# Attention mixed with a spectral filter: the score tiles lend one PSUM bank each instead of two, the last chunk's transposes move from PSUM to SBUF, and the order of the work is planned anew

## The chip, the cores and the metric

The kernel runs on one core of one Trainium2 chip. The number that counts is the device time of one execution in microseconds (us), and less is better. A core has engines that run side by side, each with its own queue of instructions that it works off strictly in order: PE (TensorE, matrix products into PSUM), ACT (ScalarE), DVE (VectorE), POOL (GpSimd) and SP, which here issues most DMAs. They wait for each other through semaphores. PSUM is the memory that PE writes; the kernel uses all of its eight banks of 128 x 512 float32.

## The reference

For an input `x` of 2048 tokens with 448 features, the result is `g * a + (1 - g) * b`, token by token:

```python
g = sigmoid((x * gate_w).sum(-1, keepdims=True))
qkv = (x @ wqkv).reshape(B, S, 3, 16, 28)             # 16 heads of 28 features
scores = einsum("bhqd,bhkd->bhqk", q, k) * 28 ** -0.5
a = (softmax(scores) @ v) @ wo                         # full attention, no mask
X = rfft2(x.astype(float32), axes=(-2, -1))
b = irfft2(X * (w_r + 1j * w_i), s=(2048, 448)).astype(bfloat16)
```

All inputs are bfloat16, and so is the result.

## The kernel before

**Attention.** The heads stand in four groups of four (`g`), the queries in four blocks of 512 (`qc`). One pair is a **chunk**, so there are 16, worked off one after the other; the last has `g` = 3 and `qc` = 3. A chunk has 64 **units**: 16 blocks of 128 keys times four heads. For each unit PE makes a 128 x 512 block of scores (L1166), one of two engines turns it into weights, and PE adds `V` times the weights into the bank `psV` (L1249). One round of scores (`scores`) fills one of the two tiles `psA0` and `psA1`, which have **two banks each**; ACT then makes the exponentials of both banks with one instruction of 128 x 1024 (L1189). When DVE has room, the round takes a third or fourth unit into single banks `psX0` to `psX2`; DVE turns those into weights by an integer method (the "z" at L1212, which fills an SBUF tile `P`, and two "shifts" of the tile at L1232, on DVE or POOL, each of which fills a further `P`). Before the values of such a unit are complete, PE uses all three.

**The other work** goes between these rounds: the projections of queries, keys and values, the forward and inverse transforms, and at the end the output tiles. All of it lands in the banks `psX`, and `take_bank` hands out whichever is free. `spare` lists further banks that may be lent: `psV` and the banks of the `psA` tiles. They are lent while the exponentials have not started, and the `psA` banks again when the last scores are out: an exponential that ends after that puts its tile's banks on the free list (`add_exp`, in `done`).

**The end of the program.** There are 16 output tiles of 128 tokens, t = 4 `qc` + b. A tile needs 20 matmuls of 32 x 448 into one bank: four for each of the four head groups (`Wo` against `qT`, which holds the normalised attention by then), and four that add the transform (`bufA`). It is then scaled and copied to SBUF (L865 on DVE, L867 on ACT; tiles `fin0` to `fin3`, and for t = 12 to 15 the halves of `T12_0` and `T12_1`) and stored by a DMA. Tiles 12 to 15 are **late**: 16 of their matmuls are made ahead, and the four of the last head group follow when chunk 15 is normalised. That last step is `finale`: DVE transposes `psV` in two halves of 256 columns, takes reciprocals of the sums, multiplies them by the odds of the gate, multiplies the halves by the result, and transposes back into `qT3_3` (L1361 to L1370). The transposed halves lie in two `psX` banks that are taken for good. While `finale` is under way (`self.final`), DVE takes no other work, so output tiles are scaled by ACT. POOL's last work is the 16 sums and 16 differences of the inverse transform that fill `bufA` (L826, L828).

**What sets the order.** Nothing in the program text does. `plan` runs a small event-driven model of the engines while the program is built: each engine, when free, takes the ready step with the best priority, with the rules of `pick`, `dispatch` and `want_D`. The numbers in `TUNE` are due times and thresholds of those rules. The instructions are then written in the order in which the model started them, so any change of a rule, of a bank or of a number can reorder everything behind it. A tile framework adds the semaphore waits, by the tiles that an instruction reads and writes.

Of the kernel before, what the change touches and what calls it, by code (L numbers as in the profile page):

```python
# [16 lines left out]
ALU = mybir.AluOpType  # L17
# [11 lines left out]
ONE = DH  # L29
# [139 lines left out]
class Unit:  # L169
    __slots__ = ("bank",)  # L170

    def __init__(self):
        self.bank = None


TUNE = dict(T0=14686.546, LC=22185.379, late=11458.875, pzmin=5, urg=6, lastd=1, dt1=1308.304, dt2=934.424, minx2=1,
            poolt=7236.982, th=152.929, pw=94.522, pt=5990.959, ph=174.007, slack=205.092, q0a=0.939, q0b=0.915, q0n=1.28,
            v0=1.985, v1=0.481, vr=0.337, va=4.36, vb=0.452, kb=-3.17, ks=0.299, kn=-2.187, qb=-1.855, qs=0.176, qn=-2.498,
            gate=-0.848, fo=0.11, fos=0.629, fa=1.907, fas=0.25, sp=2.701, sps=4189.909, fc=7.462, fcs=0.275, fp=11.206,
            fps=0.212, fsd=44318.209, ow=15952.526, ows=2033.1, u8=-4896.554, u12=21653.512, relx=-4760.365, mc=46.01)  # L180

ENGINES = ("PE", "ACT", "DVE", "POOL", "SP")
LAT = {"PE": 230.0, "ACT": 170.0, "DVE": 150.0, "POOL": 80.0, "SP": 0.0}
# [12 lines left out]
class Kernel:  # L196
# [522 lines left out]
    def transform(self, at):  # L719
# [161 lines left out]
    def plan(self):  # L881
        self.order = []
        self.out_d = {}
        self.norm_d = {}
        self.late = {}
        self.norms = []
        self.seq = 0
        self.evq = []
        self.now = 0.0
        self.free_at = {e: 0.0 for e in ENGINES}  # L890
        self.port_until = 0.0
        self.ready = {e: [] for e in ENGINES}
# [48 lines left out]
        left = [o.name for o in self.ops if not o.started and o.engs]  # L941
        assert not left, (t, self.pos, self.pv, left[:30])
# [244 lines left out]
    def add_exp(self, p, us, i, slot):  # L1187
        n = len(us)
        e = self.op("exp", {"ACT": t_act(QW * n)}, lambda o: self.nc.scalar.activation(  # L1189
            out=self.P[slot][:, 0:n, :], in_=self.PSA[i][:, 0:n, :], func=ACT.Exp, scale=math.log(2.0) / UNIT), [p], -1e9)  # L1190
# [159 lines left out]
    def finale(self, p, g, qc):  # L1350

        nc = self.nc
        n0 = len(self.ops)
        self.final = 2
        for h in range(2):
            u = Unit()
            u.bank = self.take_bank()
            cs = slice(256 * h, 256 * h + 256)
            R, tmp = self.Rsm[h][:].rearrange("p j b -> p (j b)")[:, 0:8], self.nq[h][:, 0:256]
            blk = lambda x: x.rearrange("p (c d) -> p c d", d=32)  # L1360
            e = self.ev(f"t1{h}", {"DVE": 340.0}, lambda e, u=u, cs=cs: nc.vector.transpose(out=u.bank[:, 0:256], in_=self.PSV[:, cs]),  # L1361
                        [p], -2e9 + 10 * h)
            e = self.ev(f"t2{h}", {"DVE": 130.0}, lambda e, u=u, R=R: nc.vector.reciprocal(
                out=R, in_=u.bank[:, ONE:256:32]), [e], -2e9 + 10 * h + 1)
            e = self.ev(f"t3{h}", {"DVE": 70.0}, lambda e, R=R, h=h: nc.vector.tensor_tensor(
                out=R, in0=R, in1=self.oddsT[:, 1, 8 * h:8 * h + 8], op=ALU.mult), [e, self.o_oddsT], -2e9 + 10 * h + 2)
            e = self.ev(f"t4{h}", {"DVE": 340.0}, lambda e, u=u, R=R, tmp=tmp: nc.vector.tensor_tensor(
                out=blk(tmp), in0=blk(u.bank[:, 0:256]), in1=R.rearrange("p (c o) -> p c o", o=1).to_broadcast([128, 8, 32]), op=ALU.mult),
                [e], -2e9 + 10 * h + 3)
            e = self.ev(f"t5{h}", {"DVE": 340.0}, lambda e, cs=cs, tmp=tmp: nc.vector.transpose(  # L1370
                out=self.qT[g][qc][:, cs], in_=tmp), [e], -2e9 + 10 * h + 4)
            e.kind = "t5"
            self.finals(qc, h, e)
        self.wake(n0)
# [47 lines left out]
```

## Time and profile before

| what | value |
|---|---|
| time, median of 3 runs | 378.99 us (377.62 to 381.48) |
| the profiled execution's own time | 378.07 us |
| its span, first to last instruction | 376.3 us |
| ACT busy | 359.7 us (96%) |
| PE busy | 354.2 us (94%) |
| DVE busy | 333.5 us (89%) |
| POOL busy | 259.2 us (69%) |
| TensorE clock granted, mean | 1.000 |

The profile is of one execution. Between its span and its time lie 1.8 us outside the first and last instruction. Engines overlap, so shares do not add up to one; what an engine's work is worth depends on whether another waits for it. Instructions of ACT and DVE are pipelined: one starts before the one ahead has ended, so the step from start to start is shorter than the duration of one.

### The profile page before, as it was taken

To read this page: it belongs to the slowest core of one execution; us is meant where nothing else is said; L and a number is where in the kernel's file an instruction comes from. 1 tells how busy PE (TensorE), PEld (TensorE's weight loads), DVE (VectorE), ACT (ScalarE), POOL (GpSimd) and SP (SyncE) were. 2 spreads that over 40 slices of the span, in tenths; PEclk is the share of its full clock that TensorE was granted. 3 is DMA by queue.
4 is the path that set the end of the run, shared out by engine and by line. 5 is a ranking of instruction groups with operands and counts; after the bars stand their busy time and mean duration, and the time that the engine had idled before them with its cause. 6 is when DMAs were issued, how large, how long until landed. Compare 5 with 4: busy or idle time off the path is not lost.

```text
span 376.3 us, 13601 instructions
## 1 busy us (share of the span) xinstructions
PE 354.2 (94%) x5656; PEld 132.8 (35%) x5656; DVE 333.5 (89%) x604; ACT 359.7 (96%) x403; POOL 259.2 (69%) x292
## 2 busy tenths in 40 slices
PE   7999999999999999999989999999989889999994
PEld 5552224335333343233333333232324323332342
DVE  1679999999999999999999999998999989999970
ACT  4999999999999999999999999999999999999962
POOL 5555677766777865668766678687778876775780
PEclk9999999999999999999999999999999999999999
DMA  8701120211855532202212212112100100101012
GB/s 239 163 3 4 5 36 4 60 22 46 99 63 89 75 58 38 57 3 67 53 48 57 64 46 60 47 29 68 31 17 17 24 11 2 33 13 54 26 64 75
DMA packets 43493, 18.55 MB, mean 49 GB/s; under 512 B 29876, under 2 KB 41580, under 8 KB 43432
## 3 DMA queue, kind: packets, MB, share of 16 engines
q1 hardware_dynamic: 42680, 17.54, 23.0%
q8 instruction: 44, 0.72, 0.9%
q10 hardware_dynamic: 752, 0.15, 0.2%
q14 instruction: 17, 0.14, 0.1%
HBM read 13.71 MB, written 2.07 MB: 42 GB/s over the span
## 4 chain that ended last, share of the span: by engine, by line
PE 60%; ACT 24%; DVE 9%; issue 4%; DMA 1%; POOL 0%; SPq 0%; ACTq 0%; DVEq 0%
ACT P L1189 23%; PE psA L1166 21%; PE psX L355 20%; PE psV L1249 16%; DVE P L1212 5%; PE psA L355 2%; DVE P L1232 1%; DMA bufA<-in_A_x_dram 1%; PE psX L458 1%; POOL P L1232 0%; PE psX L1166 0%; DVE kT L557 0%; ACT fin L867 0%; DVE Oraw L367 0%; DVE VT L834 0%
## 5 line engine op out<-in xcount | busy, mean ns | idle before, releaser
L1189 ACT ACTIVATE P<-psA 128x1024 bf16<-128x1024 f32 x379 | 348.8, 1125 | 1.1 <-PE psX L1166 1.1
L1232 POOL TENSOR_SCALAR P<-P 128x1024 int16<-128x1024 int16 (+1 forms) x164 | 168.5, 1029 | 64.8 <-DVE P L1232 22.6
L1212 DVE TENSOR_SCALAR P<-psX 128x512 int16<-128x512 f32 x267 | 177.6, 684 | 14.5 <-PE psX L1166 12.1
L1166 PE MATMUL psA<-qT,kT 32*128 32x512 bf16 x757 | 146.5, 383 | 12.2 <-ACT P L1189 10.8
L1249 PE MATMUL psV<-P,V 128*32 128x512 bf16 x1558 | 129.9, 384 | 0.9 <-DVE P L1212 0.7
L1166 PE MATMUL psX<-qT,kT 32*128 32x512 bf16 x267 | 93.4, 384 | 0.0
L1166 PEld LDWEIGHTS <-kT 32*128 32x128 bf16 x1024 | 41.6, 91 | 133.3 <-issue 129.5
L1249 PEld LDWEIGHTS <-V 128*32 128x32 bf16 x1558 | 32.7, 94 | 45.5 <-issue 41.3
L1232 DVE TENSOR_SCALAR P<-P 128x1024 int16<-128x1024 int16 (+1 forms) x108 | 45.3, 422 | 0.4
L355 PE MATMUL psX<-xT,Wp 112*32 112x512 bf16 (+2 forms) x528 | 40.7, 377 | 0.5 <-ACT xT L370 0.5
L1313 POOL TENSOR_TENSOR qT<-Oraw,Rbc 128x512 bf16<-128x512 f32 x14 | 17.9, 1277 | 3.2 <-DVE P L1232 2.0
L789 DVE TENSOR_TENSOR T<-psX,Wst 128x900 bf16<-128x900 f32 x16 | 17.3, 1084 | 0.2
L355 PEld LDWEIGHTS <-Wp 112*32 112x32 bf16 x528 | 11.0, 94 | 14.4 <-issue 12.3
L746 POOL TENSOR_TENSOR VT<-bufA 128x900 bf16<-128x900 bf16 x8 | 14.4, 1794 | 1.8 <-DVE P L1232 1.1
L355 PEld LDWEIGHTS <-xT 112*32 112x32 bf16 x768 | 12.6, 96 | 6.9 <-issue 6.4
L797 POOL TENSOR_TENSOR bufA<-T 128x225 bf16<-128x225 bf16 x16 | 9.8, 613 | 6.0 <-DVE P L1232 5.5
L355 PEld LDWEIGHTS <-VT 113*32 113x32 bf16 (+2 forms) x512 | 10.0, 95 | 8.8 <-issue 8.1
L355 PE MATMUL psX<-IV,bufA 128*32 128x256 bf16 (+1 forms) x256 | 12.2, 275 | 0.2 <-DVE P L1212 0.2
L355 PE MATMUL psX<-Wo,qT 128*32 128x448 bf16 x160 | 12.3, 356 | 0.0
L795 POOL TENSOR_TENSOR bufA<-T 128x225 bf16<-128x225 bf16 x16 | 9.0, 562 | 4.5 <-PE psX L1166 2.2
L826 POOL TENSOR_TENSOR bufA<-bufB 128x225 bf16<-128x225 bf16 x16 | 9.3, 583 | 3.7 <-DVE P L1232 2.9
L834 DVE CAST VT<-psX 113x512 bf16<-113x512 f32 x16 | 10.8, 676 | 1.0 <-PE psX L355 1.0
(106 smaller groups left out, 288.2 us busy)
## 6 DMA issues: line engine op xcount, KB each, us to landing
Rbc<-dR SPq DMA_DIRECT2D x14, 256.0 KB
IV<-c_IV SPq DMA_DIRECT2D x16, 128.0 KB
bufA<-bufB SPq DMA_DIRECT2D x16, 112.5 KB
S<-c_S SPq DMA_DIRECT2D x16, 96.0 KB
bufA<-in_A_x_dram SPq DMA_DIRECT2D x3, 448.0 KB
out_dram<-fin SPq DMA_DIRECT2D x12, 112.0 KB
Wst<-in_B_w_r_dram SPq DMA_DIRECT2D x7, 112.5 KB
Wst<-in_B_w_i_dram SPq DMA_DIRECT2D x7, 112.5 KB
```

The costliest lines, as they stand in the source:

```text
L355: self.nc.tensor.matmul(o[c:c + n], lhsT=w[:, c:c + n], rhs=r, start=start, stop=stop, tile_position=(0, c), skip_group_check=True)
L746: fs.append(self.ev(f"fo{tg}{k}", {"POOL": 1860.0}, lambda e, ts=ts, k=k, op=op, lo=lo, hi=hi: nc.gpsimd.tensor_tensor(out=self.XF[:, ts, ...
L789: e = self.ev(f"fm{g}", {"DVE": t_dve(2 * F2)}, lambda e, u=u, T=T, g=g: nc.vector.tensor_tensor(out=T[:].rearrange("p r (a f) -> p r a f" ...
L797: y2 = self.ev(f"fz{g}", {"POOL": 580.0}, lambda e, T=T, g=g: nc.gpsimd.tensor_tensor(out=self.bufA[:, g, F:F2], in0=T[:, 1, 0:F], in1=T[: ...
L826: es = [self.ev(f"fs{t}", {"POOL": 580.0}, lambda e, t=t, even=even, odd=odd: nc.gpsimd.tensor_tensor(out=y[:, t, 0:F], in0=even, in1=odd, ...
L834: self.nc.vector.tensor_copy(out=self.VT[:, :, :, :, 8 * g:8 * g + 8].rearrange("p c r t k -> p (c r t) k"), in_=u2.bank[0:HF, :].rearrang ...
L1166: nc.tensor.matmul(out, lhsT=self.kT[g][32 * j:32 * j + 32, 128 * kt:128 * kt + 128], rhs=self.qT[g][qc][32 * j:32 * j + 32, :], start=Tru ...
L1189: e = self.op("exp", {"ACT": t_act(QW * n)}, lambda o: self.nc.scalar.activation(out=self.P[slot][:, 0:n, :], in_=self.PSA[i][:, 0:n, :], ...
L1212: e = self.op("z", {"DVE": t_dve(QW)}, lambda o: self.nc.vector.tensor_scalar(out=zt.bitcast(I16), in0=ub.bank, scalar1=float(ZBASE), scal ...
L1232: return en.tensor_scalar(out=self.P[q[1 + s]][:, 0:n, :].bitcast(I16), in0=self.P[q[0]][:, 0:n, :].bitcast(I16), scalar1=1.0, scalar2=flo ...
L1249: self.nc.tensor.matmul(self.PSV[32 * j:32 * j + 32, :], lhsT=self.V[:, kt, 4 * (i // NQ) + j, :], rhs=rhs, start=first, stop=False, tile_ ...
L1313: n = self.ev(f"n7_{c}", {"POOL": 1350.0}, lambda e: nc.gpsimd.tensor_tensor(out=self.qT[g][qc][:], in0=self.Oraw[r][:], in1=self.Rbc[r][: ...
```

## The change

Four edits. First, `spare` lists one bank of each `psA` tile (index 0) instead of both, and an exponential that ends after the last scores frees that bank alone. Second, `finale` no longer takes two banks: the transposed halves go to the SBUF tiles `Rbc0` and `Rbc1` (float32, used until then for the normalisations of earlier chunks), and the transposes wait for the last two of those normalisations. Third, the bank `psV` goes to the free list when the second transpose has read it. Fourth, nine numbers of `TUNE` are different (one of them, `mc`, is read nowhere), so the planner makes another order.

```diff
-TUNE = dict(..., urg=6, ...
-            poolt=7236.982, th=152.929, ...
-            v0=1.985, v1=0.481, vr=0.337, va=4.36, ..., qs=0.176, qn=-2.498,
-            ..., sp=2.701, ..., fcs=0.275, ...
-            ..., ow=15952.526, ..., mc=46.01)
+TUNE = dict(..., urg=7, ...
+            poolt=7236.982, th=-150.489, ...
+            v0=1.985, v1=0.481, vr=0.337, va=3.546, ..., qs=0.13, qn=-1.791,
+            ..., sp=2.768, ..., fcs=0.277, ...
+            ..., ow=11736.011, ..., mc=56.007)
...
-        self.spare = [self.PSV[:]] + [self.PSA[i][:, k, :] for i in (1, 0) for k in range(2)]
-        for b, o in zip(self.spare, ("V", 1, 1, 0, 0)):
+        self.spare = [self.PSV[:]] + [self.PSA[i][:, 0, :] for i in (1, 0)]
+        for b, o in zip(self.spare, ("V", 1, 0)):
...
-                self.freeX += [self.PSA[i][:, k, :] for k in range(2)]
+                self.freeX.append(self.PSA[i][:, 0, :])
...
+        t1 = []
         for h in range(2):
-            u = Unit()
-            u.bank = self.take_bank()
             cs = slice(256 * h, 256 * h + 256)
+            X = self.Rbc[h][:, 0:256]
...
-            e = self.ev(f"t1{h}", {"DVE": 340.0}, lambda e, u=u, cs=cs: nc.vector.transpose(out=u.bank[:, 0:256], in_=self.PSV[:, cs]),
-                        [p], -2e9 + 10 * h)
+            e = self.ev(f"t1{h}", {"DVE": 340.0}, lambda e, X=X, cs=cs: nc.vector.transpose(out=X, in_=self.PSV[:, cs]),
+                        [p] + self.norms[-2:], -2e9 + 10 * h)
+            t1.append(e)
+            if h:
+                e.on_done = lambda: self.freeX.append(self.PSV[:])
...
-                out=blk(tmp), in0=blk(u.bank[:, 0:256]), in1=R.rearrange(...
+                out=blk(tmp), in0=blk(X), in1=R.rearrange(...
```

The new lines push the later ones down by three: what is L1363 to L1370 before is L1366 to L1373 after.

Counted over the whole program, ACT has 378 exponentials instead of 379, and DVE has 269 z instead of 267. Of the shifts, DVE has 116 instead of 108 and POOL 158 instead of 164; of the squares of keys (L373), DVE has 6 instead of 10 and POOL 6 instead of 2. PE has four more matmuls for values (1562 instead of 1558). The first 1,670 instructions on PE, 59 on DVE and 62 on ACT are the same.

Three places at the end of the program follow. A name like `psA1_160` is bank tile `psA1` (the number behind it is the program's own), `qT3_3` is head group 3 of query block 3, and `qT0_3` head group 0 of it.

On ACT, the last exponential and the output tiles behind it. Before:

```order
L1189 ACTIVATE P17_112<-psA0_159 128x1024
L867 ACTIVATE fin1_155<-psA1_160,omg_151 128x448
L867 ACTIVATE fin2_156<-psA1_160,omg_151 128x448
L867 ACTIVATE fin3_157<-psA0_159,omg_151 128x448
L867 ACTIVATE T12_0_128<-psA0_159,omg_151 128x448
L867 ACTIVATE T12_0_128<-psX0_161,omg_151 128x448
L867 ACTIVATE T12_1_129<-psA1_160,omg_151 128x448
```

After:

```order
L1189 ACTIVATE P1_96<-psA1_160 128x1024
L867 ACTIVATE fin3_157<-psX0_161,omg_151 128x448
L867 ACTIVATE fin1_155<-psX1_162,omg_151 128x448
L867 ACTIVATE fin2_156<-psA0_159,omg_151 128x448
L867 ACTIVATE fin3_157<-psA1_160,omg_151 128x448
L867 ACTIVATE T12_0_128<-psX2_163,omg_151 128x448
L867 ACTIVATE T12_0_128<-psX0_161,omg_151 128x448
L867 ACTIVATE T12_1_129<-psV_164,omg_151 128x448
```

Before, five of the six output tiles on ACT come from the two `psA` tiles, two and three in a row from the same pair. After, each comes from another bank than the one ahead of it, no pair is used twice, and there are seven: tile 7 (`fin3` from `psX0`) is scaled behind the last exponential too.

On PE, the matmuls of the late tiles 12 to 15: for each stretch of equal target and source its first row stands here. Before:

```order
L355 MATMUL psA0_159<-Wo_71,qT0_3_78 32x448
...
L355 MATMUL psX0_161<-Wo_71,qT0_3_78 32x448
...
L355 MATMUL psA0_159<-Wo_71,qT3_3_90 32x448
...
L355 MATMUL psA1_160<-Wo_71,qT0_3_78 32x448
...
L355 MATMUL psX0_161<-Wo_71,qT3_3_90 32x448
...
L355 MATMUL psA1_160<-Wo_71,qT3_3_90 32x448
```

After:

```order
L355 MATMUL psX2_163<-Wo_71,qT0_3_78 32x448
...
L355 MATMUL psX0_161<-Wo_71,qT0_3_78 32x448
...
L355 MATMUL psX2_163<-Wo_71,qT3_3_90 32x448
...
L355 MATMUL psV_164<-Wo_71,qT0_3_78 32x448
...
L355 MATMUL psX0_161<-Wo_71,qT3_3_90 32x448
...
L355 MATMUL psX1_162<-Wo_71,qT0_3_78 32x448
...
L355 MATMUL psV_164<-Wo_71,qT3_3_90 32x448
...
L355 MATMUL psX1_162<-Wo_71,qT3_3_90 32x448
```

The sequence of steps is the same, tiles 12, 13, the end of 12, 14, the end of 13, 15, and the ends of 14 and 15. Before, tiles 14 and 15 share `psA1`, and tile 12 shares `psA0` with tile 11; after, the four tiles have four banks.

On DVE, `finale` and the last output tile. Before:

```order
L865 TENSOR_SCALAR fin0_154<-psX0_161,omg_151 128x448
L1361 STREAM_TRANSPOSE psX2_163<-psV_164 128x256
L1361 STREAM_TRANSPOSE psX1_162<-psV_164 128x256
L1363 RECIPROCAL Rsm0_136<-psX2_163 128x8
...
L1365 TENSOR_TENSOR Rsm0_136<-Rsm0_136,oddsT_148 128x8
...
L1367 TENSOR_TENSOR nq0_92<-psX2_163,Rsm0_136 128x256
...
L1370 STREAM_TRANSPOSE qT3_3_90<-nq0_92 128x256
...
L865 TENSOR_SCALAR T12_1_129<-psA1_160,omg_151 128x448
```

After:

```order
L865 TENSOR_SCALAR fin0_154<-psX2_163,omg_151 128x448
L1361 STREAM_TRANSPOSE Rbc0_132<-psV_164 128x256
L1361 STREAM_TRANSPOSE Rbc1_133<-psV_164 128x256
L1366 RECIPROCAL Rsm0_136<-Rbc0_132 128x8
...
L1368 TENSOR_TENSOR Rsm0_136<-Rsm0_136,oddsT_148 128x8
...
L1370 TENSOR_TENSOR nq0_92<-Rbc0_132,Rsm0_136 128x256
...
L1373 STREAM_TRANSPOSE qT3_3_90<-nq0_92 128x256
...
L865 TENSOR_SCALAR T12_1_129<-psX1_162,omg_151 128x448
```

The same ten instructions stand in the same order; the transposed halves are in SBUF, and so the multiplication L1370 has two inputs from SBUF where L1367 had one from PSUM. On both sides the last instruction writes the second half of `T12_1`, whose first half ACT writes just ahead of it.

More of the change, by code (lines that the diff above doesn't have):

```diff
@@ L173, in __init__ @@
         self.bank = None
[L176 to L180, printed above, removed]
+TUNE = dict(T0=14686.546, LC=22185.379, late=11458.875, pzmin=5, urg=7, lastd=1, dt1=1308.304, dt2=934.424, minx2=1,
+            poolt=7236.982, th=-150.489, pw=94.522, pt=5990.959, ph=174.007, slack=205.092, q0a=0.939, q0b=0.915, q0n=1.28,
+            v0=1.985, v1=0.481, vr=0.337, va=3.546, vb=0.452, kb=-3.17, ks=0.299, kn=-2.187, qb=-1.855, qs=0.13, qn=-1.791,
+            gate=-0.848, fo=0.11, fos=0.629, fa=1.907, fas=0.25, sp=2.768, sps=4189.909, fc=7.462, fcs=0.277, fp=11.206,
+            fps=0.212, fsd=44318.209, ow=11736.011, ows=2033.1, u8=-4896.554, u12=21653.512, relx=-4760.365, mc=56.007)
 ENGINES = ("PE", "ACT", "DVE", "POOL", "SP")
@@ L1354, in finale @@
         self.final = 2
+        t1 = []
         for h in range(2):
-            u = Unit()
-            u.bank = self.take_bank()
             cs = slice(256 * h, 256 * h + 256)
+            X = self.Rbc[h][:, 0:256]
             R, tmp = self.Rsm[h][:].rearrange("p j b -> p (j b)")[:, 0:8], self.nq[h][:, 0:256]
             blk = lambda x: x.rearrange("p (c d) -> p c d", d=32)
-            e = self.ev(f"t1{h}", {"DVE": 340.0}, lambda e, u=u, cs=cs: nc.vector.transpose(out=u.bank[:, 0:256], in_=self.PSV[:, cs]),
-                        [p], -2e9 + 10 * h)
-            e = self.ev(f"t2{h}", {"DVE": 130.0}, lambda e, u=u, R=R: nc.vector.reciprocal(
-                out=R, in_=u.bank[:, ONE:256:32]), [e], -2e9 + 10 * h + 1)
+            e = self.ev(f"t1{h}", {"DVE": 340.0}, lambda e, X=X, cs=cs: nc.vector.transpose(out=X, in_=self.PSV[:, cs]),
[3 more added lines that the diff above has]
+                e.on_done = lambda: self.freeX.append(self.PSV[:])
+            e = self.ev(f"t2{h}", {"DVE": 130.0}, lambda e, X=X, R=R: nc.vector.reciprocal(
+                out=R, in_=X[:, ONE:256:32]), [e], -2e9 + 10 * h + 1)
             e = self.ev(f"t3{h}", {"DVE": 70.0}, lambda e, R=R, h=h: nc.vector.tensor_tensor(
                 out=R, in0=R, in1=self.oddsT[:, 1, 8 * h:8 * h + 8], op=ALU.mult), [e, self.o_oddsT], -2e9 + 10 * h + 2)
-            e = self.ev(f"t4{h}", {"DVE": 340.0}, lambda e, u=u, R=R, tmp=tmp: nc.vector.tensor_tensor(
-                out=blk(tmp), in0=blk(u.bank[:, 0:256]), in1=R.rearrange("p (c o) -> p c o", o=1).to_broadcast([128, 8, 32]), op=ALU.mult),
+            e = self.ev(f"t4{h}", {"DVE": 340.0}, lambda e, X=X, R=R, tmp=tmp: nc.vector.tensor_tensor(
+                out=blk(tmp), in0=blk(X), in1=R.rearrange("p (c o) -> p c o", o=1).to_broadcast([128, 8, 32]), op=ALU.mult),
                 [e], -2e9 + 10 * h + 3)
```

## The prediction

> **What bounds the kernel now.** I read the page's busy shares first, then its chain that ended last, then the end of the program engine by engine.
>
> ```profile
> span 376.3 us, 13601 instructions
> PE 354.2 (94%) x5656; PEld 132.8 (35%) x5656; DVE 333.5 (89%) x604; ACT 359.7 (96%) x403; POOL 259.2 (69%) x292
> PE 60%; ACT 24%; DVE 9%; issue 4%; DMA 1%; POOL 0%; SPq 0%; ACTq 0%; DVEq 0%
> L1189 ACT ACTIVATE P<-psA 128x1024 bf16<-128x1024 f32 x379 | 348.8, 1125 | 1.1 <-PE psX L1166 1.1
> L1212 DVE TENSOR_SCALAR P<-psX 128x512 int16<-128x512 f32 x267 | 177.6, 684 | 14.5 <-PE psX L1166 12.1
> L1166 PE MATMUL psA<-qT,kT 32*128 32x512 bf16 x757 | 146.5, 383 | 12.2 <-ACT P L1189 10.8
> ```
>
> Three engines are near full, and the chain names PE most. But the 379 exponentials leave ACT only 1.1 us idle, and PE waits 10.8 us for them before scores, while they wait 1.1 us for PE. In the middle of the program the stream of exponentials sets the pace, and PE is filled to it. How fast the stream runs is seen when it is cut into stretches of 24 exponentials (busy time of PE, PE's weight loads, DVE, ACT and POOL in each):
>
> ```profile
> 35.98:58.62 22.64, 21.43 (x277) 6.14 (x269) 21.92 (x42) 22.32 (x27) 15.32 (x15) 1.00 0.23 18
> 58.62:80.71 22.09, 21.60 (x426) 8.45 (x415) 20.94 (x43) 22.09 (x26) 15.95 (x15) 1.00 0.14 31
> 212.92:234.81 21.89, 21.02 (x311) 7.35 (x307) 20.78 (x36) 21.89 (x25) 16.25 (x19) 1.00 0.25 64
> 301.01:322.92 21.91, 19.72 (x271) 7.03 (x271) 20.12 (x39) 21.91 (x25) 14.75 (x17) 1.00 0.04 6
> ```
>
> 24 exponentials take 21.9 us in a good stretch, 0.912 each, and 22.64 in the worst of these, where DVE is busy 21.92 of it. So the middle has little left to win, and it can lose where DVE fills up.
>
> The end is another matter. The first row here, from ACT's timeline (start, us, what), gives the last exponential's end: 349.51 + 13.06 = 362.57. I count the end from there. The second fence is the chain in order of time, with its short pieces left out:
>
> ```profile
> 349.51 13.06 ACT L1189 ACTIVATE P<-psA 128x1024 bf16<-128x1024 f32 x14
> ```
>
> ```profile
> 363.45 1.34 PE psA L355 x24
> ...
> 364.82 0.64 ACT fin L867
> ...
> 365.50 2.10 PE psA L355 x40
> ...
> 367.63 0.64 ACT fin L867
> ...
> 368.31 0.56 PE psA L355 x8
> ...
> 369.63 0.95 PE psA L355 x20
> ...
> 370.77 1.16 PE psA L355 x24
> ...
> 371.95 0.64 ACT T L867
> 372.62 0.68 DVE T L865
> ```
>
> PE finishes at 370.77 + 1.16 = 371.93 (+9.35), ACT scales tile 14, DVE tile 15, and the span ends at 376.3 (+13.7). PE's work is cut twice by ACT: 364.79 to 365.50 and 367.60 to 368.31, 0.71 us each. The waits name it:
>
> ```profile
> PE psA L355 <- ACT fin L867: 1.5, 2, 0.7
> ACT fin L867 <- PE psA L355: 3.8, 3, 2.2
> DVE T L865 <- ACT T L867: 6.2, 1, 6.2
> ```
>
> Tiles 9 and 10 lie in the two banks of `psA1`, and 11 and 12 in those of `psA0`. PE, in the middle of tile 10, waits until ACT has read tile 9, and ACT had not begun tile 9 until PE had stopped in tile 10. The waits go by the pair, not by the bank.
>
> **The change, part by part.** *The pairs are not shared any more.* With one bank lent per pair, no output tile has a neighbour. The two stops of PE go: 2 x 0.71 = 1.42 us. What is late next is PE itself. A tile costs it 0.95 us (the row of 20 matmuls above). From the order after, seven tiles (9 to 15) stand behind the last values, 7 x 0.95 = 6.65. Ahead of the last values it now also has tile 7, 0.95 us, which it can start only when the scores and eight more value matmuls are out. Before, PE turned to tile 9 here:
>
> ```profile
> 360.84 0.39 PE L1166 MATMUL psA<-qT,kT 32*128 32x512 bf16 x2
> 361.16 0.56 PE L355 MATMUL psX<-Wo,qT 128*32 128x448 bf16 x8
> 361.55 1.47 PE L1249 MATMUL psV<-P,V 128*32 128x512 bf16 x24
> 362.85 0.36 PE L355 MATMUL psA<-Wo,qT 128*32 128x448 bf16 x2
> 363.07 0.38 PE L1249 MATMUL psV<-P,V 128*32 128x512 bf16 x2
> ```
>
> The last scores end at 361.16, -1.41 from the last exponential. After the change, 12 matmuls of tile 8 (0.57), eight of values (0.4) and tile 7 (0.95) follow, until +0.5; then six last value matmuls (0.4), until +0.9, which puts their end at +1.1 and `finale` at about +1.15 (before: values end at 363.45, +0.88). Seven tiles from +0.9 end at +7.55, with the last matmul's 0.36 us instead of 0.19 at about +7.7. Against +9.35 that is **1.65 us** less. Bounds: the 28 matmuls between 362.85 and 364.79 took 1.94 us where 7 x 0.19 = 1.33 were to be expected; if that happens again, or ACT is late once more (0.6), only 0.4 to 1.0 is won; if tile 7 is done earlier, 2.3.
>
> *ACT has seven tiles instead of six.* Each takes 0.64, and PE delivers one per 0.95, so ACT keeps up; tile 7 is scaled from +0.55. `fin3` serves tiles 7 and 11, so tile 11 must wait until tile 7 is stored: by the last store below, 376.3 - 373.3 = 3.0 us from the scaling's end to the program's, so about +4.2, and PE delivers tile 11 at +3.8. Half a microsecond, hidden, since tile 12 is due at +5.5.
>
> *The last two scalings.* DVE still writes the half of `T12_1` beside ACT's, so its wait for ACT can stay: 0.64 + 0.68, then the store, as before. I count nothing.
>
> *Transposes in SBUF.* The timeline has these rows of `finale` now (DVE), then the one case of the same multiplication from SBUF, 512 wide, then POOL's instruction beside that one and POOL's last:
>
> ```profile
> 363.49 0.80 DVE L1361 STREAM_TRANSPOSE psX<-psV 128x256 f32<-128x256 f32 x2 [1.03 <-PE psV L1249]
> 364.98 0.74 DVE L1367 TENSOR_TENSOR nq<-psX,Rsm 128x256 bf16<-128x256 f32 x2
> 365.64 0.75 DVE L1370 STREAM_TRANSPOSE qT<-nq 128x256 bf16<-128x256 bf16 x2
> 353.61 1.06 DVE L1334 TENSOR_TENSOR nq<-Rbc,Rsm 128x512 bf16<-128x512 f32 x1
> 353.55 0.58 POOL L828 TENSOR_TENSOR bufA<-bufB 128x223 bf16<-128x223 bf16 x1
> 366.05 0.57 POOL L828 TENSOR_TENSOR bufA<-bufB 128x223 bf16<-128x223 bf16 x1
> ```
>
> `finale` lasts 363.49 to 366.39, 2.90 us. The transpose into SBUF I take as equal. The multiplication of 256 columns is 0.41 from PSUM (0.74 for the two, overlapped); from SBUF it lies between that and the 1.06 of the 512 wide row, so the pair costs 0 to 1.3 us more. I take 0.5, nearer the low end, since half the columns are moved. `finale` then ends at 1.15 + 2.90 + 0.5 = +4.55, at worst +5.35. PE needs its first half behind tiles 9, 10, 11 and the first parts of 12 and 13, 23 groups of 0.19 from +0.9, at +5.3. So the cover is 0.75 us, and the loss at worst 0.05: nothing.
>
> The L1334 row began 0.06 us behind POOL's L828 and would fit a stop until that ended at 354.13, and 0.54 us of work. The Trainium skill, "SBUF — State Buffer", § Who interferes with whom, states this as a rule: a DVE instruction with two SBUF inputs contends with a GpSimd instruction that reads SBUF, and the second to issue blocks until the first is through. It speaks against the change: POOL is at its sums until 366.62 here, so each of the two multiplications could stand up to 0.57 us behind one, and `finale` would end at about +5.2 by the rule, +4.05 without it. The sum is the same by both, as PE comes at +5.3.
>
> *One exponential fewer.* 0.91 us off ACT's stream; its two units go to DVE as two z. DVE also gets eight more shifts and loses four squares:
>
> ```profile
> L1232 DVE TENSOR_SCALAR P<-P 128x1024 int16<-128x1024 int16 (+1 forms) x108 | 45.3, 422 | 0.4
> L373 DVE TENSOR_TENSOR sqk<-kT 128x512 bf16<-128x512 bf16 x10 | 4.2, 418 | 0.0
> 28.26:361.50 333.24, 319.41 (x4900) 112.18 (x4892) 314.45 (x566) 332.10 (x367) 237.86 (x262) 1.00 0.22 41
> ```
>
> 2 x 0.68 + 8 x 0.42 - 4 x 0.42 = 3.0 us more, against 333.24 - 314.45 = 18.8 us in which DVE is idle in the middle. On average it fits, so I count **-0.91**.
>
> *The new order.* The rows do not say where it stalls. The view of the exponentials' line has the first and the last start:
>
> ```profile
> L1189 ACT ACTIVATE P<-psA x379: 602/1127/1268, 10.5 to 361.4; 128x1024 bf16<-128x1024 f32 x190
> ```
>
> At 0.912 the 378 steps would take 344.7 us; they took 350.9. The 6.2 us are stalls and ACT's other work, so less than that can be won, and what can be lost is bounded only by the worst stretch. I count 0, with -2 to +4 (the 0.7 us that the stretch at 35.98 lost, in six of the fifteen stretches).
>
> **Sum**: the profiled execution's 378.07 - 1.65 - 0.91 = **375.5 us**. That execution lies 0.9 below the median of 378.99, whose runs spread over 3.9, so the same gain would read 376.4 by the median; I stay with 375.5.
>
> **The rivals.**
> *The tail keeps its length.* ACT's stop is followed by another: `finale` reaches PE late, or POOL's sums, or ACT's seven tiles. For it: three engines end within 6 us of each other, and POOL's last sum ended at 366.62, +4.05. Against it: the covers above, and tile 15 needs its sum only at +6.4. Then 378.07 - 0.91 = 377.2, and with a little of the gain 376.8.
> *The stream runs better too.* The worst stretches (22.64, 22.09) become 21.9: two more us, 373.5. For it: the losses are early, at 28 to 59 us, behind the first instruction that differs. Against it: what causes them, the head's work, is all still there.
> *Slower: DVE becomes the bound of the stream.* PE works in order, so a score into a `psX` bank that DVE has not read stops the next scores for ACT as well. The place is the middle, from 36 us on. It decides once a stretch of 24 exponentials holds over 21.9 us of DVE work, as at 35.98: that stretch cost 0.7 over the good one. DVE has 3.0 us more, and where it falls is set by the new order. With 22.64 in twelve stretches, 12 x 0.7 = 8.4, less the 2.6: 383.9; in eight, 381. For it: the stretches hold 20.1 to 21.9 already. Against it: 18.8 us idle, which three hardly use up.
> *It does not do what it says.* The banks that are lent change at the end alone, and the rows show them there; so this is only the first rival.
>
> **How the numbers follow.** Forecast 0.47 (374.3 to 376.6), the tail keeps its length 0.2 (376.6 to 378.5), stream better too 0.18 (372.5 to 374.3), slower 0.15 (379 to 384). The range 372.8 to 380.0 leaves out the worst of the last and the best of the third. A gain or loss of about 1% (3.8 us) is what this kernel's runs can tell from no change. Faster by over 1% holds the third rival and a third of the forecast's width, 0.34; slower by over 1% most of the fourth, 0.13; the rest, 0.53, is within.
>
> **What would show it.** Right: between the last exponential and PE's last matmul 7.7 us instead of 9.35; no wait of PE for `fin` on `psA`; tile 15 still scaled behind ACT's tile 14; the last exponential near 361.7. Wrong: stretches of 24 exponentials of 22.5 us and more, PE waiting for DVE before scores, or PE standing at the last head group's matmuls because `finale` is late.

## The result, and the profile after

The changed kernel takes **377.33 us** (median of 22 runs, 375.62 to 384.62) against 379.31 (22 runs, 377.62 to 381.71) for the kernel before: a ratio of 0.9948, 95% interval 0.9926 to 0.997. It is faster, by a little over half of what the prediction's 375.5 against 378.99 (0.9908) meant. The range held the time; the likeliest case's own range (374.3 to 376.6) did not.

The profiled execution took 378.21 us. From its page, the span, the busy times, and the granted clock in 40 slices:

```profile
span 376.3 us, 13634 instructions
PE 359.2 (95%) x5660; PEld 135.7 (36%) x5660; DVE 334.8 (89%) x609; ACT 359.9 (96%) x403; POOL 258.2 (69%) x290
...
PEclk9999999999999999999999999999999969999999
```

The span is what it was before, 376.3. Whoever compares the two pages finds no gain at all. It has to be cut in three: the head (to the first exponential), the stream of exponentials, and the tail (from the end of the last one). The view of the exponentials' line gives the first and last start, ACT's timeline the end (358.96 + 5.76 = 364.72):

```profile
L1189 ACT ACTIVATE P<-psA x378: 601/1160/1294, 11.6 to 363.5; 128x1024 bf16<-128x1024 f32 x189
```

```profile
358.96 5.76 ACT L1189 ACTIVATE P<-psA 128x1024 bf16<-128x1024 f32 x6
```

| part | before | after | difference |
|---|---|---|---|
| head, to the first exponential | 10.47 | 11.61 | +1.14 |
| stream, first to last start | 350.97 | 351.89 | +0.92 |
| last exponential | 1.13 | 1.23 | +0.10 |
| tail: to the end of PE | 9.33 | 8.06 | -1.27 |
| tail: from there to the end of the last scaling | 1.40 | 0.80 | -0.60 |
| tail: from there to the end of the span | 2.96 | 2.70 | -0.26 |

**The tail** is 2.13 us shorter. All waits of ACT and DVE, in the list of waits from 360 us on (line that waits, line waited for: us, times, longest); the rows left out are POOL's and those of weight loads that wait for nothing the profile shows:

```profile
DVE T L865 <- PE psX L355: 3.0, 1, 3.0
ACT fin L867 <- PE psX L355: 1.8, 2, 0.9
...
ACT T L867 <- PE psX L355: 1.3, 2, 1.0
DVE Rbc L1361 <- PE psV L1249: 1.3, 1, 1.3
DVE P L1212 <- PE psX L1166: 1.3, 2, 0.8
...
DVE fin L865 <- PE psX L355: 0.8, 1, 0.8
...
ACT fin L867 <- PE psA L355: 0.7, 2, 0.4
...
ACT T L867 <- PE psV L355: 0.3, 1, 0.3
```

PE no longer waits for `fin`; it is in no row as the one that waits, and ACT and DVE wait for PE alone. Nor does DVE wait for ACT any more before tile 15. DVE's timeline, and ACT's last instruction:

```profile
367.14 0.97 DVE L1368 TENSOR_TENSOR Rsm<-Rsm,oddsT 128x8 f32<-128x8 f32 x2
368.04 1.20 DVE L1370 TENSOR_TENSOR nq<-Rbc,Rsm 128x256 bf16<-128x256 f32 x2
369.15 0.76 DVE L1373 STREAM_TRANSPOSE qT<-nq 128x256 bf16<-128x256 bf16 x2
372.90 0.68 DVE L865 TENSOR_SCALAR T<-psX,omg 128x448 bf16<-128x448 f32 x1 [2.98 <-PE psX L355]
```

```profile
372.64 0.63 ACT L867 ACTIVATE T<-psV,omg 128x448 bf16<-128x448 f32 x1 [0.31 <-PE psV L355]
```

DVE starts tile 15 at 372.90, while ACT is at tile 14 until 373.27. `finale` ends at 369.15 + 0.76 = 369.91, +5.18 from the last exponential.

**The stream** lost time in one place. Stretches of 3.41 us (length, busy time of PE, PE's weight loads, DVE, ACT and POOL, then the granted clock):

```profile
296.05:299.46 3.41, 3.22 (x51) 1.14 (x44) 3.35 (x7) 3.41 (x5) 2.64 (x3) 1.00 0.16 58
299.46:302.88 3.42, 2.04 (x26) 0.76 (x23) 3.11 (x7) 3.42 (x5) 2.58 (x3) 1.00 0.08 26
302.88:306.29 3.41, 3.41 (x38) 1.16 (x38) 2.59 (x6) 2.66 (x3) 2.09 (x2) 0.50 0.00 0
306.29:309.70 3.41, 3.41 (x28) 0.64 (x24) 2.66 (x5) 2.59 (x4) 1.29 (x2) 0.50 0.09 5
```

For 6.8 us PE runs at half clock, is busy all the time, and ACT waits for it. Two later profiles of the same order without this (order alone, and transposes in PSUM, below) have streams of 349.48 and 349.34, so it cost 2.5 us; undisturbed, the new order's stream is 1.5 to 1.6 shorter than the old one's.

**The head** has the same instructions before and after. PE's timeline of the kernel before (start, us), then after:

```profile
0.99 2.53 PE L417 MATMUL psX<-nq 128*128 128x128 bf16 x22 [0.99 <-DVE nq L413]
4.05 0.95 PE L458 MATMUL psX<-ident,bufA 128*112 128x128 bf16 x8 [0.53 <-DMA bufA<-in_A_x_dram]
5.30 0.65 PE L458 MATMUL psX<-ident,bufA 128*112 128x128 bf16 x8 [0.30 <-DMA bufA<-in_A_x_dram]
6.40 2.26 PE L355 MATMUL psX<-xT,Wp 112*32 112x512 bf16 x48 [0.45 <-ACT xT L370]
```

```profile
0.99 2.53 PE L417 MATMUL psX<-nq 128*128 128x128 bf16 x22 [0.99 <-DVE nq L413]
3.98 2.28 PE L458 MATMUL psX<-ident,bufA 128*112 128x128 bf16 x16 [0.47 <-DMA bufA<-in_A_x_dram]
6.51 3.30 PE L355 MATMUL psX<-xT,Wp 112*32 112x512 bf16 x48 [0.25 <-ACT xT L370]
```

The 48 projections take 2.26 us in one and 3.30 in the other: the granted clock becomes full at 4.7 us in the first execution and at 9.3 in the second.

So three questions: what of the change shortened the tail, whether the head is luck, and why the clock was halved.

### The profile page after: what moved, and what is told of

Its sections match the earlier page's. It is cut to its first block, busy times and chain, and to the rows that moved or that the text cites. A ratio compares the mean times of both kernels' runs of the same rounds, so it can differ in the third digit from the quotient of the medians.

```text
span 376.3 us, 13634 instructions
## 1 busy us (share of the span) xinstructions
PE 359.2 (95%) x5660; PEld 135.7 (36%) x5660; DVE 334.8 (89%) x609; ACT 359.9 (96%) x403; POOL 258.2 (69%) x290
## 4 chain that ended last, share of the span: by engine, by line
PE 56%; ACT 30%; DVE 7%; issue 5%; DMA 1%; SPq 0%; ACTq 0%; DVEq 0%
ACT P L1189 30%; PE psX L355 20%; PE psA L1166 19%; PE psV L1249 14%; DVE P L1212 4%; DVE P L1232 1%; DMA bufA<-in_A_x_dram 1%; PE psX L458 1%; DVE T L789 1%; PE psV L355 1%; PE psA L355 1%; DVE VT L834 0%; PE psX L1166 0%; DVE Oraw L367 0%; PE psV L458 0%
## 5 line engine op out<-in xcount | busy, mean ns | idle before, releaser
L1232 POOL TENSOR_SCALAR P<-P 128x1024 int16<-128x1024 int16 (+1 forms) x158 | 163.2, 1034 | 65.8 <-DVE P L1232 23.2
L1212 DVE TENSOR_SCALAR P<-psX 128x512 int16<-128x512 f32 x269 | 179.7, 684 | 16.3 <-PE psX L1166 14.2
L1249 PE MATMUL psV<-P,V 128*32 128x512 bf16 x1562 | 132.8, 388 | 0.4 <-DVE Oraw L367 0.3
L1166 PE MATMUL psX<-qT,kT 32*128 32x512 bf16 x269 | 94.6, 387 | 0.0
L1166 PEld LDWEIGHTS <-kT 32*128 32x128 bf16 x1024 | 42.7, 91 | 135.0 <-issue 130.7
L1232 DVE TENSOR_SCALAR P<-P 128x1024 int16<-128x1024 int16 (+1 forms) x116 | 49.8, 431 | 0.4
L355 PE MATMUL psX<-xT,Wp 112*32 112x512 bf16 (+2 forms) x528 | 41.9, 390 | 0.2 <-ACT xT L370 0.2
L355 PE MATMUL psX<-Wo,qT 128*32 128x448 bf16 x208 | 16.5, 355 | 0.0
L355 PEld LDWEIGHTS <-xT 112*32 112x32 bf16 x768 | 12.6, 96 | 8.3 <-issue 7.6
L355 PE MATMUL psX<-IV,bufA 128*32 128x256 bf16 (+1 forms) x256 | 11.6, 275 | 0.0
L369 POOL COPY Wp<-Wst 112x448 bf16<-112x448 bf16 x7 | 3.7, 559 | 11.5 <-DMA Wst<-in_A_wqkv_dram 6.6
```

Of the source, the lines that this page charges most:

```text
L355: self.nc.tensor.matmul(o[c:c + n], lhsT=w[:, c:c + n], rhs=r, start=start, stop=stop, tile_position=(0, c), skip_group_check=True)
L1166: nc.tensor.matmul(out, lhsT=self.kT[g][32 * j:32 * j + 32, 128 * kt:128 * kt + 128], rhs=self.qT[g][qc][32 * j:32 * j + 32, :], start=Tru ...
L1212: e = self.op("z", {"DVE": t_dve(QW)}, lambda o: self.nc.vector.tensor_scalar(out=zt.bitcast(I16), in0=ub.bank, scalar1=float(ZBASE), scal ...
L1232: return en.tensor_scalar(out=self.P[q[1 + s]][:, 0:n, :].bitcast(I16), in0=self.P[q[0]][:, 0:n, :].bitcast(I16), scalar1=1.0, scalar2=flo ...
L1249: self.nc.tensor.matmul(self.PSV[32 * j:32 * j + 32, :], lhsT=self.V[:, kt, 4 * (i // NQ) + j, :], rhs=rhs, start=first, stop=False, tile_ ...
```

## Experiments: which part shortened the tail

Theory: two output tiles in the two banks of one `psA` tile wait for each other, and one bank per pair is what counts. Rival: the other edits (transposes in SBUF, `psV` lent, the order) free PE.

**One bank per pair alone**, old order, transposes in PSUM:

```diff
-        self.spare = [self.PSV[:]] + [self.PSA[i][:, k, :] for i in (1, 0) for k in range(2)]
+        self.spare = [self.PSV[:]] + [self.PSA[i][:, 0, :] for i in (1, 0)]
...
-                self.freeX += [self.PSA[i][:, k, :] for k in range(2)]
+                self.freeX.append(self.PSA[i][:, 0, :])
```

> The order of before; one bank of each pair is lent, nothing else: transposes in two psX banks, the values' bank not lent, so that only three banks carry seven tiles. Theory (sharing decides): no stop for a pair, and a bank is free again in time since PE needs 0.95 us a tile and ACT 0.64: tail 11.2 to 11.8, as with all three edits, ratio 0.994. Rival (the number of free banks decides): PE waits for banks, tail 13 to 14, no gain.

**All edits to the banks and to `finale`, old order** (the diff of the change without `TUNE`):

> The three edits of banks and transposes, with the numbers of TUNE as before: the order of every engine is that of the kernel before, and only the banks of the last tiles and the transposes' target differ. Theory (a pair of banks that two output tiles share makes PE and ACT stop for each other): the stretch from the last exponential's end to the end of the span falls from 13.7 us to 11.2 to 11.6, no wait of PE for fin is left, the stream is that of before; 2.2 us faster, ratio 0.994. Rival (the gain is in the new order of the stream): the same time as before, within 0.3%.

**Transposes in SBUF and `psV` lent, old order, both banks of a pair still lent** (the diff of the change in `finale` alone):

> The order of before; the transposes go to SBUF and the values' bank is lent, but both banks of each pair are lent as before. Three psX banks are free at the end now, so tiles 11 and 12 share one pair and 13 and 14 the other. Theory (sharing decides): one or two stops remain, tail 12.0 to 12.8, 0.9 to 1.7 us faster than before. Rival (the number of free banks decides): as with all three edits, tail 11.2 to 11.6.

**The new order alone** (the diff of the change in `TUNE` alone):

> The numbers of TUNE alone: the order of the changed kernel, with both banks of a pair lent and the transposes in PSUM. Here only tiles 10 and 11 share a pair. Theory: one stop of 0.7 us returns against the changed kernel (tail 12.2 to 12.6 instead of 11.6), the stream is that of the changed kernel, about 1.3 us shorter than before where the clock is full; 1.5 to 2.5 us faster than before. Rival (the order gives nothing but one exponential): 0.9 less from the stream and a tail as before, ratio 0.998. Rival (the order makes PE denser and so the clock is held back more): slower than before by 0.5 us or more in the runs with a clock under 1.

**The new order with one bank per pair, `finale` as before** (the change without its diff in `finale`):

> The new order with one bank per pair, but with the last transposes in PSUM as before and the values' bank not lent; only where those transposes lie differs from the changed kernel. Theory: the SBUF transposes and the values' bank buy nothing, so the tail is 11.4 to 11.7 us as in the changed kernel (11.56), the pair of multiplications in the last step takes 0.74 us again instead of 1.20, and the last step ends about half a microsecond earlier after the last exponential. Rival: seven output tiles on three free banks instead of four make PE wait for a bank, and the tail is 12 us or more. The time is that of the changed kernel to within 0.4 us by the theory, 0.5 to 1 us above by the rival.

Measured, with the changed kernel once more (each beside the kernel before, whose median was 379.12 and 379.09 in the two sessions; ratios with 95% intervals; tail and PE's end in us from the end of the last exponential, in one profile each):

| kernel | order | one bank per pair | SBUF, `psV` | tail | PE's end | stream | median | ratio |
|---|---|---|---|---|---|---|---|---|
| before | old | no | no | 13.69 | +9.33 | 350.97 | 379.1 | 1 |
| one bank per pair | old | yes | no | 11.43 | +7.50 | 350.96 | 377.15 | 0.9961 (0.993 to 0.9992) |
| all bank edits | old | yes | yes | 11.43 | +7.50 | 350.93 | 377.68 | 0.9968 (0.9933 to 1.0003) |
| SBUF and `psV` | old | no | yes | 12.52 | +8.57 | 352.15, half clock | 378.73 | 0.9978 (0.9944 to 1.0013) |
| order alone | new | no | no | 13.29 | +9.79 | 349.48 | 379.09 | 1.0006 (0.9972 to 1.0039) |
| PSUM transposes | new | yes | no | 11.55 | +8.06 | 349.34 | 376.78 | 0.9962 (0.9938 to 0.9986) |
| changed kernel again | new | yes | yes | 11.55 | +8.06 | 350.33, half clock | 376.78 | 0.9945 (0.9915 to 0.9976) |

One bank per pair, alone, has the whole tail: 2.26 us, and the two edits to `finale` add nothing to it in either order (11.43 and 11.43; 11.55 and 11.55). Its list of waits begins with these rows, and PE is in none as the one that waits for ACT:

```profile
DVE T L865 <- PE psA L355: 3.8, 1, 3.8
ACT fin L867 <- PE psA L355: 1.9, 1, 1.9
ACT T L867 <- PE psA L355: 1.4, 2, 1.1
```

The tails came out as expected, the times gained less (0.9961 for one bank per pair and 0.9968 for all bank edits, where 0.994 was expected). The intervals of the four rows with one bank per pair overlap. The changed kernel was expected once more near 378, with three quarters of its runs at a lower clock (below); it came out at 376.78, with 7 of 12. Where pairs are still shared, the waits for the neighbour stay; the list of waits at the end of SBUF and `psV` alone, then that of the order alone:

```profile
PE psA L355 <- ACT fin L867: 0.7, 1, 0.7
```

```profile
ACT fin L867 <- DVE Rsm L1363: 2.0, 1, 2.0
...
PE psA L355 <- ACT fin L867: 0.7, 1, 0.7
PE psA L355 <- DVE psA L1361: 0.6, 1, 0.6
```

In the second, `finale`'s transposes got one bank of a pair whose other bank held an output tile, so PE, DVE and ACT waited in a ring. I had expected a tail of 12.2 to 12.6 there; it is 13.29.

The multiplication from SBUF, in the old order from PSUM and then from SBUF (both with one bank per pair), then in the new order from PSUM:

```profile
366.94 0.74 DVE L1367 TENSOR_TENSOR nq<-psX,Rsm 128x256 bf16<-128x256 f32 x2
```

```profile
366.59 1.57 DVE L1370 TENSOR_TENSOR nq<-Rbc,Rsm 128x256 bf16<-128x256 f32 x2
```

```profile
366.36 0.41 DVE L1367 TENSOR_TENSOR nq<-psX,Rsm 128x256 bf16<-128x256 f32 x1
366.70 0.41 DVE L1367 TENSOR_TENSOR nq<-psA,Rsm 128x256 bf16<-128x256 f32 x1
```

The pair takes 0.74 us from PSUM in the old order and 0.75 in the new (366.36 to 367.11), and 1.57 or 1.20 from SBUF while POOL makes its sums. In the 1.20 the first multiplication takes 0.86 beside POOL's last sum, and the second, with POOL idle, 0.41, as from PSUM. PE's end does not move, so the cover that the prediction named is there.

## Experiments: the head

**Six more matmuls at the start.** PE multiplies 22 tiles of nothing before the inputs are there, then is idle for 0.3 to 0.8 us. With 28 it isn't:

```diff
-        mms = [(128, lambda: nc.tensor.matmul(...))
+        mms = [(128, lambda i=i: [nc.tensor.matmul(...)
+                                  for k in range(1 if i < WARMUPS - 1 else 7)])
```

On the changed kernel, and on the old order with one bank per pair:

> The changed kernel with six more of the 128 x 128 matmuls that PE runs before the inputs are there, so that PE has no idle time of 0.5 to 0.8 us between them and the first projections. Theory: PE is at half clock until about 10 us because that gap starts its wait for full clock anew; without the gap the clock is full from about 5 us, the first exponential starts at 10.5 us instead of 11.6 to 12.5, and the time is 1.0 to 1.5 us below the changed kernel's. Rival: the clock's start has nothing to do with the gap; then the first exponential stays at 11.6 to 12.5 and the time is unchanged to 0.3 us, or up to 0.4 longer by the matmuls added.

> The old order with one bank per pair and nothing else of the change, with the same six matmuls at the start. Theory: tail 11.4 us as with one bank per pair alone, first exponential at 10.5 us instead of 12.4, clock stretches as rare as in the kernel before (a third of the runs): median 375.5 to 376.2. Rival (the start doesn't depend on the gap): median 376.9 to 377.4, the first exponential at 12.4.

PE's timeline of the first:

```profile
0.99 3.17 PE L417 MATMUL psX<-nq 128*128 128x128 bf16 x28 [0.99 <-DVE nq L413]
3.95 1.81 PE L459 MATMUL psX<-ident,bufA 128*112 128x128 bf16 x16
6.20 2.22 PE L355 MATMUL psX<-xT,Wp 112*32 112x512 bf16 x48 [0.45 <-ACT xT L370]
```

The projections take 2.22 us. The first exponential starts at 10.23 and 10.32; in the two later kernels with these matmuls at 10.33 and 10.40. Of the ten profiles without them, two show 10.35 and 10.47, the other eight 11.6 to 12.5. So the early head of the kernel before was luck, worth 1.1 us and more. The times: 376.28 (9 runs, ratio 0.9939, 0.9911 to 0.9967) and 377.10 (12 runs, 0.9935, 0.9904 to 0.9966). Both gained less than expected: the first is 0.5 below the changed kernel beside it, where 1.0 to 1.5 was expected, and the second was expected at 375.5 to 376.2. Only the runs at full clock show the gain: their medians go from 376.57 (10 runs of the changed kernel) to 374.72 (2), and in the old order from 376.87 (8) to 375.64 (5). The other runs had the half clock, which is the third question.

## Experiments: the halved clock

Each run lists its mean granted clock; below 0.9965 I count it as halved somewhere in the middle. (3.41 us at half clock take 0.0045 off it; half clock behind PE's end alone took 0.0025 at most in a profile.) This was so in 23 of 98 runs of the kernel before, in 20 of 48 of the old order with other banks or more matmuls at the start, and in 56 of 79 of the new order (the control below among them). Such runs are longer by 2.6 us (medians of the kernel before: 381.43 against 378.84) and 1.5 (changed kernel: 378.04 against 376.57).

My theory was that PE's busy time in the 3.41 us ahead decides. In the profiles seen by then, the clock was halved behind windows with PE busy 60 to 69%, as 299.46 to 302.88 above, and all other windows at full clock had 71% and more. So I filled that hole, and as a control put the same matmuls elsewhere:

```diff
+        self.round = getattr(self, "round", -1) + 1
+        again = mms[:1] if 309 <= self.round <= 315 else []
...
-            for (c, kt, j), out in mms:
+            for (c, kt, j), out in again + mms:
```

> The changed kernel, with one matmul of scores written twice in each of the seven rounds of exponentials 309 to 315 (299.7 to 305.1 us), where PE has its least busy 3.4 us. The output is unchanged. Theory: the clock is halved behind a stretch of 3.41 us in which PE is busy less than about 70% (0.60 to 0.69 in the four profiles that show it, 0.71 and more in all others); the new order has such a hole at 299.5 us, 0.59 deep, and seven matmuls of 0.215 us raise it to 0.8. Then nearly no run has a mean granted clock below 0.9965 (24 of 34 in the changed kernel), and the median is 376.3 to 376.7 with few runs above 378. Rival: the half clock comes by itself or by heat; then two thirds of the runs show it still and the median is unchanged or up to 0.5 longer by the matmuls added.

> The same seven extra matmuls in the changed kernel, but in the rounds of exponentials 286 to 292 (278.4 to 284.0 us), where PE is busy over 0.73 of each 3.4 us. Theory: the hole at 299.5 us is left, so about two thirds of the runs have a mean granted clock below 0.9965, as in the changed kernel, and the median is 376.8 to 378. Rival: it is the extra work anywhere that changes it; then the share falls here as it does with the hole filled.

> The changed kernel with both: the hole at 299.5 us filled, and six more matmuls at the start. Theory: the head gains 1.3 to 2.0 us as in the run with these matmuls alone (first exponential at 10.2), no half clock in the middle: 374.3 to 375.0 median, below both kernels by over 1 us. Rival: the matmuls at the start help only sometimes or the hole still halves the clock: 375.8 to 376.5.

> The old order with one bank per pair, six more matmuls at the start, and the same filling in eight rounds (exponentials 309 to 316, 298.1 to 304.4 us); its hole there is 0.63 deep. Against the new order with both, only the order differs. Theory: without half clock the new order is worth the 1.5 us that the streams of exponentials differ by (349.4 and 350.9): 375.5 to 376.3 here, and nearly no run with a mean granted clock below 0.9965 (7 of 12 without the filling). Rival: the orders differ by less once the clock is full, and the time is within 0.5 us of the new order with both.

| kernel | halved runs | median | ratio |
|---|---|---|---|
| hole filled | 8 of 12 | 377.57 | 0.9954 (0.9922 to 0.9985) |
| filled elsewhere | 8 of 12 | 377.65 | 0.9962 (0.9933 to 0.9992) |
| filled, more matmuls at the start | 7 of 12 | 377.48 | 0.994 (0.9909 to 0.9972) |
| old order, both | 2 of 9 | 376.14 | 0.993 (0.9903 to 0.9958) |

**The theory fell.** In the new order the halved runs are as many as in the control. The third kernel's profile shows why: its windows are

```profile
298.95:302.36 3.41, 2.83 (x29) 0.72 (x28) 2.88 (x7) 3.41 (x4) 2.09 (x2) 1.00 0.06 20
302.36:305.78 3.42, 3.42 (x37) 1.16 (x37) 2.31 (x5) 2.26 (x3) 2.09 (x2) 0.50 0.00 0
```

PE is busy 83% of the first window, and the clock is halved all the same. It has few matmuls, 29, though other windows with as few stayed full. All six halvings in the profiles begin near one place of the program, behind a window that starts at 298 to 304 us.

So I formed another, from the fourteen profiles: what counts is **how much of the array is in use**. Each matmul is counted with its rows times columns in use (in the trace) over 128 x 128, and with the time of its columns at full clock: the 128 x 128 matmuls at the start begin 0.107 us apart at half clock, so 0.053 at full. A score matmul of 512 columns uses 32 rows, a quarter, so it too counts 0.053 us, though PE is busy with it for 0.2 or more. The clock changes only at steps of 3.413 us, so each profile tells its windows:

| share of the array in one window | what the clock did next |
|---|---|
| 0.27, 0.28, 0.28, 0.32, 0.33, 0.35 | halved (six profiles; 0.35 is the filled one) |
| over 0.36, and ten between 0.329 and 0.36 | stayed full (all other windows before PE's last tiles) |
| at half clock, up to 0.344 in all but one (0.365) | stayed half |
| at half clock, 0.34, 0.347, 0.372 and above (to 0.48) | became full |

One value near 0.34 sorts nearly all of the 1,500 windows, in the head too; the few on the wrong side are off by 0.03 at most. The window's place against the program differs from run to run. If it lands anywhere with equal chance, a window below 0.34 is met in 29% of the runs of the old order and 70% of the new one (holes of 0.27 at 300 us and 0.31 at 192); measured 71% in the new order, but in the old one 23% for the kernel before and 42% for its variants (29% together). These shares hang on the value: with 0.33 they are 18% and 53%, with 0.35 56% and 88%. And no profile shows a halving at 192 us; the one window below 0.34 that lay there (0.329) was followed by full clock. With the filling, by matmuls that use a quarter of the array, 51% in the new order (0.33 at 299 and the hole at 192 left) and 8% in the old; measured 15 of 24 and 2 of 9. The value was chosen from the same profiles, so this is a fit and not a test. The test, matmuls of the whole array in both holes, was not run and stays open.

The Trainium skill, "TensorE: Matmul & The Clock Gate", § What's actually happening, states that the clock is either half or full, judged in free-running windows of 3413 ns by how busy PE was. The steps of 3.413 us and the two values agree with this case's traces. That section gives an idle window as the reason for half clock; here the clock fell behind windows in which PE was busy 60 to 83%.

In the last table the two bottom rows differ in the order, in `finale`, which added nothing above, and in one round of filling. Their runs at full clock have medians of 375.14 (5 runs) and 376.06 (7), 0.9 apart, as the streams of the two orders with the filling are at full clock (350.33 and 351.31); over all runs the old order is ahead, since 7 of 12 against 2 of 9 were halved. No kernel is shown to be faster than the changed one: the best two, 376.14 and 376.28, have intervals that overlap its own.

## Why the prediction was right and where it was wrong

- **The two stops of PE, 1.65 us: right in kind, sized too high.** Both are gone, and the runs show that sharing a pair was the whole cause (in the order before, tiles 9 and 10, 11 and 12, 14 and 15 shared one). PE's end moved by 1.27: it is at +8.06 where I had +7.7, inside the bounds. The step that was mis-sized is what lies ahead of the last values: they end at 365.79 + 0.38 = 366.17, +1.44 where I had +1.1, and from there to PE's end it is 6.6 us, as reckoned. (I also read the end of the last scores before as 361.16; the row, 360.84 + 0.39, says 361.23.) In the old order, where tile 7 is done earlier, one bank per pair alone moved PE's end by 1.83.

```profile
365.79 0.38 PE L1249 MATMUL psV<-P,V 128*32 128x512 bf16 x1
```

- **ACT's seven tiles, hidden: right.** In the list of waits ACT waits for PE alone.
- **"Its wait for ACT can stay: ... I count nothing": wrong.** I laid the 6.2 us wait of tile 15 to the shared `T12_1`, which is still shared. The wait is gone, with one bank per pair alone too, so it was the pair again (tiles 14 and 15 both lay in `psA1`). Worth 0.60. Another 0.26 behind the last scaling comes with the new order (2.70 in the order alone, 3.13 with one bank per pair in the old order, 2.96 before). The tail's sum was thus -1.65 against -2.13 measured.
- **Transposes in SBUF, nothing: right.** `finale` ended at +5.18, behind my +4.55 and within the worst case. It started 0.32 later than I had it, the multiplications by the odds (L1368) took 0.97 instead of 0.61, which they do in the new order with PSUM too (0.95), and the pair took 1.20 instead of 0.74. The pair is longer only where both inputs are in SBUF and POOL works beside it. These rows fit the Trainium skill's rule ("SBUF — State Buffer", § Who interferes with whom) on DVE instructions with two SBUF inputs beside GpSimd. The +5.2 that the prediction worked out by that rule is met by luck, since the pair has only 0.46 of the 1.1 us added there. PE's end is the same with `finale` 0.45 us earlier (PSUM transposes).
- **One exponential fewer, -0.91, and the order 0: the stream gained 1.4 and 1.5 at full clock** (order alone and PSUM transposes, with the last exponential), so the order gave another 0.5 to 0.6. DVE did not become the bound: at full clock the slowest stretch of 24 exponentials behind the start is 22.5 in the new order where it was 22.65. The profile of the changed kernel has one of 24.2, across the half clock.
- **The order's other effect was in no part of the prediction.** Nothing in my working asked how evenly PE is loaded within 3.4 us. With 71% halved runs instead of 23% to 42%, the gain of the order is given back: one bank per pair alone, in the old order, has a median of 377.15, the changed kernel 377.13 over the 34 runs of two sessions.
- **"I stay with 375.5": wrong.** The sum was made against an execution with an early head, which eight of the ten profiles without more matmuls at the start do not have. From the median of 378.99 the same gain gives 376.4, as the text said; from 379.3, 376.7. That the range still held the time is in part luck: tail and stream gained some 1.0 us more than the sum has, and the head and the half clock, which had no term, took more than that away. The last exponential, due near 361.7, ended at 364.7 by these two.
- **What stays open.** The profiles' parts add up to 3.6 us at full clock and an equal head (2.13 and 1.46), and the runs at full clock differ by 2.3 (378.84, 75 runs, and 376.57, 10 runs). Runs without a profile do not tell where their first exponential starts. Where in the clock's windows the program starts may set both the head and the halving. For the head the profiles speak for it: of the ten without more matmuls, the two with the early head have a window that starts 1.1 and 1.3 us into the span, and the eight others have it at 0.2 to 0.8 or 2.5 to 3.3 us. For the halving no run shows it, and whether it comes from the share of the array in use was fitted, not tested.
- **The rivals.** "The tail keeps its length" has the right time (377.2) with the wrong cause; "slower" and "does not do what it says" did not happen; "the stream runs better too" was true of the stream, and hidden by the clock.

## What to carry to other kernels

Where a framework tracks dependencies by tile, two independent jobs in two banks of one tile wait for each other; look at what shares a tile before spending banks, since here lending fewer banks was faster. Before summing against one profiled execution, check how its head compares with other executions. And an order that leaves a few microseconds of thin matmul work can, by the fit above, cost clock as well as the time itself: compare the granted clock over many runs.

## What was not expected of the hardware

- The granted clock was halved in the middle of a kernel whose PE is busy 95% of the span, for 3.4 or 6.8 us in the profiles, in 23% (kernel before) to 71% (new order) of the runs. PE's busy time does not sort the windows (halved behind 83% too); the share of the array in use does, with about 0.34 in 3.413 us, by a fit that no run has tested.
- The same head takes 10.35 to 12.49 us to the first exponential; six more matmuls of the full array at the start gave 10.23 to 10.40 in four of four profiles; in one of them a window of the clock starts at 0.34 us, among those of the late heads (0.2 to 0.8).
- A multiplication pair of 128 x 256 takes 0.74 us from PSUM and 1.20 or 1.57 from SBUF beside POOL's sums; one multiplication from SBUF takes 0.86 beside a sum and 0.41 with POOL idle.
